# Issue order from a list scheduler, single PSUM banks and matmuls on zeros in a fused attention and MLP kernel

## The chip, the cores and the metric

The kernel runs on one core of one Trainium2 chip. The metric is the device time of one execution in microseconds (us); lower is better. Times are medians of several executions. Ratios are the mean time of one kernel's fast runs over the mean time of the other's in the same rounds, so they are not quite the ratio of the medians quoted beside them. A ratio comes with a 95% interval.

## The reference, cut to what matters

Sliding-window attention with four sink keys (4 batches, 8 heads, 768 positions, head size 64, window 128) is followed by a two-layer MLP (512 to 2048 to 512) with a quick GELU. Inputs and output are float32; the kernel computes in float16 with float32 sums.

```
scores = q @ k.T / 8                       # per head, 768 x 768
keep   = (key < 4) | (0 <= query - key < 128)
attn   = softmax(where(keep, scores, -1e9)) @ v
x      = attn as (4 * 768) x 512
h      = x @ w_in                          # "matmul 1", 512 x 2048
g      = h * sigmoid(1.702 * h)
out    = g @ w_out                         # "matmul 2", 2048 x 512
```

## The kernel before: the parts that matter

The 3072 rows of x are eight slabs of 384. Attention is cut into 32 units: one unit is two heads of one slab, so four units feed a slab and units 0 to 7 feed slabs 0 and 1. A unit has these steps, with the engine of each:

- T: transpose q and k (TensorE), then copy to SBUF. In the first batch T is three 128x384 matmuls against a spreading matrix for each of q and k.
- S: scores A (512 columns per head) and Z (256 or 384 per head) on TensorE, then exp on ScalarE.
- mask: a multiply on VectorE and selects on GpSimd.
- V: probabilities times values (TensorE), then normalise (VectorE).
- X: transpose back (TensorE), copy into xT (VectorE).

Matmul 1 makes h in 16 parts of 128 features per slab; ScalarE's tanh and VectorE's multiply turn each into g. Matmul 2 takes 16 accumulating 128x512 matmuls per 128 rows. Casts from float32 to float16 of q, k, v and of the eight weight blocks w_0 to w_7 run mostly on GpSimd.

The program emits the instructions of each engine in a fixed order, and the traces show the engines keep to it: in the kernel before, GpSimd stands for 8.0 us before unit 4's masks with a cast behind them whose data has landed (below). That order is written by hand: a list for the first batch, then loops.

```python
steps = {
    "T": t_chunk, "S": lambda kk: (s_chunk(kk), mask_chunk(kk)), "V": av_chunk, "X": xt_chunk,
    "c": lambda m: cast_qk(m, (pool, pool)), "v": lambda m: cast_v(m, pool), "w": cast_w,
    "F": lambda f: f_pair(0, f), "G": lambda f: f_pair(1, f),     # matmul 1 of slab 0, slab 1
}
for item in (
    "T0 T1 S0 c1 T2 S1 V0 v1 T3 S2 X0 V1 w0 S3 X1 V2 w1 X2 V3 X3 "
    "F0 F2 c2 v2 F4 T4 S4 T5 F6 S5 c3 V4 v3 T6 X4 V5 S6 T7 X5 w2 S7 V6 w3 "
    "F8 X6 V7 F10 X7 F12 F14 w4 w5 G0 G2 G4 w6 w7 G6 G8 G10 G12 G14"
).split():
    steps[item[0]](int(item[1:]))
```

The eight PSUM banks that the program uses are fixed by purpose: two pairs ("pair", for scores and for two parts of matmul 1), two single banks "misc" and two "out".

```python
def pair(name):
    return psp.tile([P, 2, 512], FP32, tag="pair", name=name)      # two of them

def s_chunk(kk):
    # ... (cut)
    A = pair(f"sA{kk}")
    # ... four score matmuls (cut)
    nc.scalar.activation(out=AT[:, 0:8]..., in_=A, func=AF.Exp, scale=scale)   # both heads at once
    Z = pair(f"sZ{kk}")
    # ... (cut)

def f_pair(n, F):                      # two parts of matmul 1
    if n_f[0] % 3 < 2:
        t = pair(f"hT{n}_{F}")         # one tanh of 128x768 over both
    else:
        hT = [bank("out", f"hT{n}_{F}_{i}", (P, SLAB)) for i in range(2)]
    # ... eight matmuls, tanh, multiply (cut)
```

The softmax here doesn't subtract the row's maximum and nothing guards it: scores larger than these inputs give would overflow.

## Time and profile before

| reading | value | view |
|---|---|---|
| time, median of three runs | 265.0 us | timed runs |
| span of the profiled execution | 261.8 us | page |
| first matmul | 5.8 us | timeline |
| first matmul 1 of slab 0 | 24.6 us | timeline |
| first matmul 1 of slab 1 | 57.8 us | timeline |
| last matmul 2 issued | 257.6 us | timeline |
| ScalarE, VectorE, GpSimd busy | 48%, 50%, 39% | page |

The profile's page is the summary of one profiled execution. PE is TensorE, PEld its weight loads, DVE VectorE, ACT ScalarE, POOL GpSimd, SPq the queue that issues the loads; L and a number is a line of the program, and out<-in names what an instruction writes and reads.

The page of the kernel before, part 1 (busy time by engine) and the lines of part 2 for TensorE and its granted clock. Each digit is one fortieth of the span, 6.5 us, in tenths.

```profile
PE 233.5 (89%) x2048; PEld 132.4 (51%) x2048; DVE 129.8 (50%) x236; ACT 124.7 (48%) x184; POOL 101.6 (39%) x173
...
PE   1585867789989999999799999998999999999994
...
PEclk9987795999999999999999999999999999999999
```

TensorE is near 9 from the ninth slice on and well below in the first eight. The clock line dips in the same place: the clock records behind it stand at 0.5 from 12.0 to 15.4, 22.2 to 29.1 and 39.3 to 46.1 us. The loads move 331 GB/s from 6 to 33 us, with the DMA engines busy all that time (a share of 1.1 in the windows view), and 21 GB/s from 33 to 40 us.

The waits of TensorE in the kernel before. The columns are the waiting tile, the releasing engine and tile, then total us, number of waits and the longest.

```profile
PE tqk_0_163 L177 <- DVE qk_0_153 L147: 5.8, 1, 5.8
PE tqk_0_203 L177 <- POOL qk_1_199 L147: 2.9, 1, 2.9
PE tqk_0_522 L177 <- POOL qk_3_492 L147: 1.9, 1, 1.9
PE sZ_475 L198 <- ACT AT_468 L207: 1.5, 1, 1.5
PE hT_10_0_689 L312 <- DVE xT_79 L296: 1.4, 1, 1.4
```

All the long ones lie before 58 us. The fourth one: a score matmul (sZ) waits for an exp to hand back one of the two PSUM pairs.

The timeline of GpSimd in the kernel before (start, duration, instruction, and in brackets the idle time before it with its releaser).

```profile
26.27 0.83 POOL L154 CAST v_2_392<-v_2_117 128x768 f16<-128x768 f32 x1
35.09 0.77 POOL L252 TENSOR_SCALAR_AFFINE_SELECT AT_421<-AT_421 128x256 f16<-128x256 f16 x2 [7.99 <-ACT AT_421 L225]
39.16 0.77 POOL L252 TENSOR_SCALAR_AFFINE_SELECT AT_468<-AT_468 128x256 f16<-128x256 f16 x2 [3.30 <-ACT AT_468 L225]
39.88 1.60 POOL L147 CAST qk_3_492<-qk_3_123 128x768 f16<-128x768 f32 x2
...
47.44 1.89 POOL L95 CAST w_in_76<-w_2_130 128x2048 f16<-128x2048 f32 x1
```

GpSimd stands for 8 us behind the masks of unit 4 and for 3 us behind those of unit 5. The casts of q/k block 3 (landed about 24 us) and of weight block w_2 (issued at 21.8 us, 8.2 us to landing) wait their turn behind those masks, until 39.9 and 47.4 us.

### The profile page before, as it was taken

The numbers are of one execution on the slowest core, as the hardware profiler recorded it, in microseconds if no ns is written. First come the engines' busy times: TensorE is split into PE (matmuls) and PEld (weight loads), VectorE is DVE, ScalarE is ACT, GpSimd is POOL, SyncE is SP. The second block draws the span as 40 slices with busy tenths as digits, with TensorE's granted clock in tenths as the row PEclk, the third lists the DMA queues.
The fourth block names the chain that finished last, engine by engine and source line by source line (L and its number), as shares of the span: only waits on it lengthen the run. The fifth ranks groups of instructions, "written<-read, shape, count | busy, mean of one in ns | idle before, by whom it ended". The sixth has DMA issues, their size and how long they took to land.

```text
span 261.8 us, 5104 instructions
## 1 busy us (share of the span) xinstructions
PE 233.5 (89%) x2048; PEld 132.4 (51%) x2048; DVE 129.8 (50%) x236; ACT 124.7 (48%) x184; POOL 101.6 (39%) x173
## 2 busy tenths in 40 slices
PE   1585867789989999999799999998999999999994
PEld 0243444446545555666355555655555556654441
DVE  6255443557537543577645434677454434764000
ACT  3371472546455651656456452656555435663111
POOL 6549114875456762166612450375313520000000
PEclk9987795999999999999999999999999999999999
DMA  7999910299997111899711113999311111000222
GB/s 190 306 359 281 385 38 3 81 319 247 226 222 197 44 43 40 204 204 229 127 43 40 43 43 103 228 213 224 62 62 41 42 43 40 3 0 0 83 80 81
DMA packets 75720, 34.12 MB, mean 130 GB/s; under 512 B 64176, under 2 KB 68656, under 8 KB 75696
## 3 DMA queue, kind: packets, MB, share of 16 engines
q1 hardware_dynamic: 75552, 33.76, 50.8%
q8 instruction: 16, 0.26, 0.4%
q14 instruction: 8, 0.07, 0.1%
q10 hardware_dynamic: 144, 0.03, 0.1%
HBM read 27.49 MB, written 6.29 MB: 129 GB/s over the span
## 4 chain that ended last, share of the span: by engine, by line
PE 68%; SPq 6%; POOL 3%; DVE 2%; ACT 2%; DMA 1%; issue 1%; ACTq 0%; POOLq 0%
SPq L126 6%; PE o_2_1031 L332 1%; PE o_0_2607 L332 1%; PE o_2_2743 L332 1%; PE o_2_1907 L332 1%; PE o_4_2945 L332 1%; PE o_4_2109 L332 1%; PE o_0_1771 L332 1%; PE o_3_2846 L332 1%; PE o_1_2660 L332 1%; PE o_3_2010 L332 1%; PE o_1_1824 L332 1%; PE o_5_3444 L332 1%; PE o_2_3384 L332 1%; PE o_5_1420 L332 1%; PE o_4_3424 L332 1%
## 5 line engine op out<-in xcount | busy, mean ns | idle before, releaser
L312 PEld LDWEIGHTS <-w_in_76 128*128 128x128 f16 x512 | 50.5, 99 | 35.9 <-issue 3.9
L332 PEld LDWEIGHTS <-gT_93 128*128 128x128 f16 x48 | 4.7, 98 | 5.7
L332 PEld LDWEIGHTS <-gT_92 128*128 128x128 f16 x48 | 4.7, 98 | 5.5
L177 PE MATMUL tqk_0_163<-spread,qk_0_153 128*128 128x384 f16 x3 | 1.1, 519 | 5.8 <-DVE qk_0_153 L147 5.8
L147 POOL CAST qk_8_1479<-qk_8_1468 128x768 f16<-128x768 f32 x2 | 1.7, 826 | 10.6 <-DMA qk_8_1468<-in_q_dram 9.7
L332 PEld LDWEIGHTS <-gT_86 128*128 128x128 f16 x48 | 4.0, 98 | 3.4
L332 PEld LDWEIGHTS <-gT_90 128*128 128x128 f16 x48 | 3.9, 97 | 3.3
L332 PEld LDWEIGHTS <-gT_88 128*128 128x128 f16 x48 | 3.9, 98 | 3.3
L147 POOL CAST qk_12_2312<-qk_12_2301 128x768 f16<-128x768 f32 x2 | 1.7, 827 | 9.6 <-DMA qk_12_2301<-in_q_dram 8.6
L332 PEld LDWEIGHTS <-gT_89 128*128 128x128 f16 x48 | 3.9, 97 | 2.8
L332 PEld LDWEIGHTS <-gT_91 128*128 128x128 f16 x48 | 3.9, 97 | 2.8
L177 PEld LDWEIGHTS <-qk_0_153 128*128 128x128 f16 x12 | 1.5, 133 | 7.4 <-DVE qk_0_153 L147 5.7
L332 PEld LDWEIGHTS <-gT_87 128*128 128x128 f16 x48 | 3.8, 98 | 2.6
L332 PE MATMUL o_2_1031<-w_out_77,gT_86 128*128 128x512 f16 x16 | 4.5, 380 | 0.0
L332 PE MATMUL o_3_1157<-w_out_77,gT_87 128*128 128x512 f16 x16 | 4.5, 380 | 0.0
L332 PE MATMUL o_4_1301<-w_out_77,gT_87 128*128 128x512 f16 x16 | 4.4, 380 | 0.0
L332 PE MATMUL o_1_937<-w_out_77,gT_86 128*128 128x512 f16 x16 | 4.3, 380 | 0.0
L332 PE MATMUL o_4_2945<-w_out_77,gT_91 128*128 128x512 f16 x16 | 4.3, 380 | 0.0
L332 PE MATMUL o_4_2109<-w_out_77,gT_89 128*128 128x512 f16 x16 | 4.3, 380 | 0.0
L332 PE MATMUL o_2_2743<-w_out_77,gT_90 128*128 128x512 f16 x16 | 4.3, 380 | 0.0
L332 PE MATMUL o_2_1907<-w_out_77,gT_88 128*128 128x512 f16 x16 | 4.3, 380 | 0.0
L332 PE MATMUL o_1_1824<-w_out_77,gT_88 128*128 128x512 f16 x16 | 4.3, 380 | 0.0
(1009 smaller groups left out, 685.3 us busy)
## 6 DMA issues: line engine op xcount, KB each, us to landing
w_0_112<-in_moe_w_in_dram SPq DMA_DIRECT2D x1, 1024.0 KB, 6.7
w_1_114<-in_moe_w_in_dram SPq DMA_DIRECT2D x1, 1024.0 KB, 8.3
w_2_130<-in_moe_w_in_dram SPq DMA_DIRECT2D x1, 1024.0 KB, 8.2
w_3_132<-in_moe_w_in_dram SPq DMA_DIRECT2D x1, 1024.0 KB, 9.6
w_4_134<-in_moe_w_out_dram SPq DMA_DIRECT2D x1, 1024.0 KB, 10.2
w_5_136<-in_moe_w_out_dram SPq DMA_DIRECT2D x1, 1024.0 KB, 5.0
w_6_138<-in_moe_w_out_dram SPq DMA_DIRECT2D x1, 1024.0 KB, 5.6
w_7_140<-in_moe_w_out_dram SPq DMA_DIRECT2D x1, 1024.0 KB, 8.2
```

The costliest lines, as they stand in the source:

```text
L126: nc.sync.dma_start(dst[:, i], s[b, hs, ti : ti + P].rearrange("h s d -> s h d"))
L147: eng(dst, src)
L177: nc.tensor.matmul(tp, qk[:, t, i], spread[:, i], start=(i == 0), stop=(i == NB - 1))
L312: nc.tensor.matmul(hT[i], w_in16[:, c, bass.ts(F + i, P)], xT[n][:, c], start=(c == 0), stop=(c == NHP - 1),)
L332: nc.tensor.matmul(ops, gT[2 * b + j][:, F, bass.ts(i, P)], w_out16[:, F], start=(F == 0), stop=(F == NF - 1))
```

## The change

The intent is to keep TensorE fed in the head. A list scheduler inside the kernel replaces the hand order. Each operation has an engine, a duration, operands and a rank; the scheduler simulates the engines at build time and the kernel emits in the order that results. PSUM becomes eight interchangeable single banks, each unit's A and Z take two each, and matmul 1 runs one part at a time with its own tanh and multiply. Four casts also change engine: k of block 0 goes from ScalarE to GpSimd, q of blocks 1 and 3 from GpSimd to VectorE, k of block 3 from GpSimd to ScalarE. Where the plan shows TensorE idle before 17 us, matmuls on zeros are put in; the intent is to hold the clock up. The diff, cut to its core:

```diff
+class Plan:
+    LAG = {"PE": 0.2, "SP": 1.6}      # time from an operation's end to its result, us
+    def op(self, name, eng, dur, emit, after=(), opens=(), uses=(), rank=0.0, at=0.0, starts=()): ...
+    def order(self, idle):            # always start the operation that can start first,
+        ...                           # ties by rank; slots (banks, buffers) are taken and freed
-    def pair(name):
-        return psp.tile([P, 2, 512], FP32, tag="pair", name=name)
+    slots = dict(ps=8, qk32=4, v32=4, w32=3, qk16=4, v65=6, qkT=8, AT0=2, AT1=2, xnat=2, th=3, ...)
-        A = pair(f"sA{kk}")
-        nc.scalar.activation(out=AT[:, 0:8]..., in_=A, func=AF.Exp, scale=scale)
+        A = [new(f"A{kk}_{h}", (P, 512), FP32) for h in range(2)]
+        for h in range(2):
+            op(f"EA{kk}_{h}", "ACT", 0.5, lambda h=h: e_a(h), ...)
-    def f_pair(n: int, F: int):
+    def add_f(n: int, F: int):        # one part: F (matmuls), H (tanh), G (multiply)
+        op(f"F{nm}", "PE", 0.655, f_mm,
+           after=[f"Xc{4 * n + 3}", f"W{F // 4}"] + ([f"F{n}_{F - 1}"] if F else []), ...)
-    cast_qk(0, (dve, act))
+    add_casts(0, "DVE", "POOL", "POOL")
+    add_casts(1, "DVE", "POOL", "POOL")
+    add_casts(2, "POOL", "POOL", "POOL")
+    add_casts(3, "DVE", "ACT", "POOL")
+    def idle(eng, start, gap):
+        if eng != "PE" or gap < 0.25 or start < 1.3 or start > plan.blank_end:
+            return None
+        return 0.22, lambda: nc.tensor.matmul(
+            T["blank"], idle_in[:, 0:P], idle_in, start=True, stop=True
+        )
+    plan.blank_end = 17.0
+    for _, _, _, emit, _ in plan.order(idle):
+        emit()
... (cut: the same operations as before, wrapped in op(...))
```

The order of instructions, which a build shows without running, has the casts of w_2 and w_3 on GpSimd after the masks of units 4 and 5, unit 4's transposes and scores before and between the first parts of matmul 1, and 17 matmuls on zeros, all after the first real transpose.

## The prediction

> What bounds the kernel now. The windows view shows two regimes. From 57.8 us (first matmul of slab 1) to 257.9 us TensorE is busy almost without a break; its idle slices there sum to about 4.5 us. Before 57.8 us it is starved. Start-to-start times in the timeline price its work: four matmul-1 parts 0.65 us, a 128x512 matmul-2 0.216 us, and per attention unit 0.34 (transposes), 0.17, 0.23, 0.15 to 0.38, 0.39 to 0.55 us. With 0.98 us for the early transposes, the first 57.8 us hold only about 27.5 us of full-speed work: 30 us are lost. The waits view names the pieces: 5.8 us for the first cast, 2.9 and 1.9 us for GpSimd casts of the next q/k, 1.5 us for a PSUM pair behind an exp, 1.4 us for xT. GpSimd itself idles from 27.1 to 35.1 us, while the cast of w_2, landed at 30 us, runs only at 47.4 us; loads w_5 to w_7 stand behind those casts until 49 to 54 us.
>
> Clock: the records show 0.5 around 12.0-15.4, 22.3-29.1 and 39.3-46.2 us; the first sixteen matmul-1s took 4.8 us instead of 2.6. [...] About 5 us are lost so.
>
> What changes. (1) Order: the list scheduler casts weights as they land, starts unit 1 before unit 2's casts, and fills the head with matmul 1 of slab 0, then slab 1 beside unit 8 on. (2) Single PSUM banks: more, smaller ScalarE work. One 128x1024 exp is 1.03 us, a 128x512 one 0.60; tanh 0.81 for a pair, 0.48 single. I estimate +15 us of ScalarE busy (125 to about 140), VectorE about level. Neither is the limit, so this costs nothing on the path. (3) 17 matmuls on zeros, 0.22 to 0.43 us each, all after the first real transpose: none warms the clock before 5.8 us, and the first two may delay unit 0 by up to 1 us. They remove the half-clock dip near 12-15 us.
>
> What stays: the loads keep their order and saturate the DMA to 33 us, so w_2 cannot land much before 30 us. GpSimd's new order puts unit 5's masks behind w_2's cast, about 32.7 us. Following the order with trace durations I expect the first slab-0 matmul 1 near 22.5 us (24.6 before) and all 27.5 us of head work done by about 44 us instead of 57.8: gain 14 us. Unit 8's transposes may stall 1.5 us for w_7 and q/k casts.
>
> After that about 194.5 us of TensorE work remain (155.6 matmul 1 and 2, 24 units at 1.6). I allow 4.5 us of waits, where before took 200. The tail (3.9 us) stays. Span 44+194.5+4.5+3.9 = 247 us; run times lie 2 to 3 us above the span.
>
> Predicted 249 us, range 242 to 256. Chances: faster 0.94, same 0.05, slower 0.01.
>
> Right if: slab 1's matmul 1 starts at 41-47 us; TensorE idle after that under 5 us; clock records have no 0.5 in 12-20 us; ScalarE busy 135-145 us with TensorE no longer waiting on exp; matmul work unchanged. Wrong if: a static order that misjudges DMA or GpSimd times makes TensorE wait behind one late operand (unit 5's masks, matmul 1 on w_2, unit 8), each several us and perhaps at half clock; or ScalarE's smaller pieces hold PSUM banks so that TensorE waits in the steady part.

The sum came to 44 + 194.5 + 4.5 + 3.9 = 247 us of span and, with 2 us added, to 249. The "about 5 us" lost to the clock is no term of it, but an estimate from the half-clock records, in which the trace has TensorE busy for 13.6 of 17.1 us.

## The result and the profile after

The changed kernel takes 249.0 us (four runs, 248.2 to 250.1) against 264.8 us (four runs, with the three of the 265.0 above); the ratio is 0.9395 with an interval of 0.9344 to 0.9446. The prediction was 249.

The page of the changed kernel, the same lines as before:

```profile
PE 231.7 (94%) x2065; PEld 132.8 (54%) x2065; DVE 135.8 (55%) x282; ACT 132.0 (53%) x291; POOL 102.1 (41%) x171
...
PE   0996999989999699999999999999999999999993
...
PEclk9998999999999999999999999999999999999999
```

In the head only the first and the fourth slice, of 6.2 us each, are still low; the zeros count as busy. TensorE's instruction count grew by the 17 zeros. ScalarE's went from 184 to 291 instructions, but its busy time rose only from 124.7 to 132.0 us.

The waits of TensorE in the changed kernel; columns as before.

```profile
PE tp L324 <- DVE qk L265: 6.0, 1, 6.0
PE av L461 <- POOL AT L420: 2.5, 3, 1.9
PE xt L484 <- DVE xn L470: 0.9, 1, 0.9
PE av L461 <- DVE AT L414: 0.8, 1, 0.8
PE tp L346 <- POOL qk L270: 0.8, 1, 0.8
...
PE hT L507 <- ACT AT L388: 0.2, 1, 0.2
```

The first wait, for the first load and cast, is unchanged. The waits for casts of q/k in the head fell from 2.9 and 1.9 us to 0.4 us (not copied), and a wait for an exp is down to 0.2 us.

The timeline of GpSimd in the changed kernel:

```profile
28.03 0.77 POOL L420 TENSOR_SCALAR_AFFINE_SELECT AT<-AT 128x256 f16<-128x256 f16 x2 [3.76 <-ACT AT L394]
28.74 0.15 POOL L279 MEMSET v<- 128x12 f16 x1
28.78 0.83 POOL L280 CAST v<-v 128x768 f16<-128x768 f32 x1
29.55 1.89 POOL L253 CAST w_in<-w 128x2048 f16<-128x2048 f32 x1
32.22 0.77 POOL L420 TENSOR_SCALAR_AFFINE_SELECT AT<-AT 128x256 f16<-128x256 f16 x2 [0.78 <-ACT AT L394]
32.94 1.89 POOL L253 CAST w_in<-w 128x2048 f16<-128x2048 f32 x1
```

The masks of unit 4 come at 28.0 us instead of 35.1, and w_2 is cast at 29.6 us instead of 47.4.

The timeline of TensorE in the changed kernel around the start of slab 1:

```profile
24.10 1.48 PE L507 MATMUL hT<-xT,w_in 128*128 128x384 f16 x4
...
44.07 1.03 PE L542 MATMUL o<-w_out,gT 128*128 128x512 f16 x4
...
45.10 1.89 PE L542 MATMUL o<-w_out,gT 128*128 128x512 f16 x8
46.83 2.76 PE L507 MATMUL hT<-xT,w_in 128*128 128x384 f16 x16
```

Slab 0's first matmul 1 starts at 24.1 us, hardly earlier than before (24.6). But slab 1 starts at 46.8 us instead of 57.8, and twelve matmul 2 are done by then that the kernel before did later. At 0.2157 us each (start to start) they are worth 2.6 us, so the head's work is done at 46.83 - 2.59 = 44.2 us. From there to the last matmul 2 it takes 199.0 us, before it took 199.9. The gain in this trace is therefore 13.5 us in the head and about 1 us after it.

This split is used for every kernel below. "Head" is the start of slab 1's first matmul 1, less 0.2157 us for each matmul 2 already started. "Rest" is from there to the start of the last matmul 2. Both are read from the timeline of one profiled execution, so differences of 1 us in them are not to be trusted.

| kernel | median us | ratio to before | head | rest |
|---|---|---|---|---|
| before | 265 | 1 | 57.8 | 199.9 |
| changed | 249.0 | 0.9395 | 44.2 | 199.0 |
| changed, run again (c0) | 249.1 | 0.941 | 44.4 | 198.2 |
| e1: no zeros | 248.4 | 0.938 | 44.2 | 196.9 |
| e2: before, GpSimd's order only | 260.8 | 0.985 | 54.5 | 199.9 |
| e3: before, ScalarE per bank | 273.5 | 1.033 | 61.0 | 206.6 |
| e5: changed, in the old order | 260.6 | 0.983 | 55.9 | 197.7 |
| e6: before, head order by hand | 260.4 | 0.981 | 54.5 | 200.8 |
| e7: e6's order, single banks | 252.9 | 0.954 | 48.3 | 198.5 |
| f1: longer load allowance | 248.4 | 0.9385 | 44.8 | 198.0 |
| f2: scheduled head, old rest | 249.0 | 0.938 | 45.3 | 197.8 |
| f3a: more zeros | 249.4 | 0.940 | 44.5 | 198.2 |
| f3b: casts on ScalarE | 250.3 | 0.943 | 44.7 | 200.4 |
| f4: f2 and f3b | 248.1 | 0.935 | 44.8 | 197.8 |

### The profile page after: what moved, and what is told of

The parts are those of the page before. It is cut to its first block, busy times and chain, and to the rows that moved or that the text cites. A ratio compares the mean times of both kernels' runs of the same rounds, so it can differ in the third digit from the quotient of the medians.

```text
span 247.7 us, 5387 instructions
## 1 busy us (share of the span) xinstructions
PE 231.7 (94%) x2065; PEld 132.8 (54%) x2065; DVE 135.8 (55%) x282; ACT 132.0 (53%) x291; POOL 102.1 (41%) x171
## 4 chain that ended last, share of the span: by engine, by line
PE 72%; DMA 7%; POOL 7%; SPq 7%; ACT 2%; DVE 2%; issue 2%; ACTq 0%; POOLq 0%
PE o L542 30%; PE hT L507 25%; SPq L220 6%; DMA v<-in_v_dram 6%; PE av L461 4%; PE A L356 3%; PE tp L324 3%; PE tp L346 2%; POOL AT L420 2%; PE Z L356 2%; DMA qk<-in_k_dram 2%; PE xt L484 2%; DVE vs L587 1%; POOL w_in L253 1%; POOL v L280 1%
## 5 line engine op out<-in xcount | busy, mean ns | idle before, releaser
L507 PE MATMUL hT<-xT,w_in 128*128 128x384 f16 x512 | 92.6, 328 | 0.2 <-ACT AT L388 0.2
L542 PE MATMUL o<-w_out,gT 128*128 128x512 f16 x384 | 89.2, 379 | 0.0
L520 DVE SCALAR_TENSOR_TENSOR gT<-th,hT 128x384 f16<-128x384 f16 x128 | 67.1, 548 | 35.0 <-ACT th L513 31.6
L513 ACT ACTIVATE th<-hT 128x384 f16<-128x384 f32 x128 | 60.9, 504 | 30.1 <-PE hT L507 27.8
L507 PEld LDWEIGHTS <-w_in 128*128 128x128 f16 x512 | 47.6, 98 | 29.4 <-issue 1.4
L420 POOL TENSOR_SCALAR_AFFINE_SELECT AT<-AT 128x256 f16<-128x256 f16 (+1 forms) x72 | 35.1, 513 | 56.1 <-ACT AT L394 23.2
L542 PEld LDWEIGHTS <-gT 128*128 128x128 f16 x384 | 35.7, 98 | 38.1 <-issue 0.2
L388 ACT ACTIVATE AT<-A 128x512 f16<-128x512 f32 x64 | 34.7, 595 | 22.1 <-PE A L356 22.1
L394 ACT ACTIVATE AT<-Z 128x256 f16<-128x256 f32 (+1 forms) x64 | 24.8, 452 | 0.0
L270 POOL CAST qk<-qk 128x768 f16<-128x768 f32 x24 | 19.4, 824 | 9.4 <-PE tp L346 3.8
L414 DVE TENSOR_TENSOR AT<-AT,masks 128x1024 f16<-128x1024 f16 x20 | 16.5, 824 | 12.0 <-ACT AT L388 11.9
L356 PEld LDWEIGHTS <-qkT 64*128 64x128 f16 (+1 forms) x384 | 11.5, 93 | 11.9 <-DVE xT L491 3.0
L469 DVE RECIPROCAL rcp<-av 128x6 f32<-128x6 f32 x32 | 6.2, 194 | 17.9 <-PE av L461 17.4
(30 smaller groups left out, 131.4 us busy)
```

The costliest lines, as they stand in the source:

```text
L270: ENG[eng](dst.rearrange("p i h d -> p (i h d)"), src)
L356: nc.tensor.matmul(dst.rearrange("p (t s) -> p t s", s=P), key[hd[h]], qkT(kk)[hd[h], 0, i0 : i0 + ni], start=True, stop=True,)
L388: nc.scalar.activation(out=T[at_][:, 4 * h : 4 * h + 4].rearrange("p a s -> p (a s)"), in_=T[f"A{kk}_{h}"], func=AF.Exp, scale=scale,)
L394: nc.scalar.activation(out=T[at_][:, 8 + SZ[g] * h : 8 + SZ[g] * (h + 1)].rearrange("p a s -> p (a s)"), in_=T[f"Z{kk}_{h}"][:, 0 : SZ[g] ...
L420: nc.gpsimd.affine_select(out=ap, in_=ap, pattern=[[0, ap.shape[1]], [sgn, P]], compare_op=ALU.is_ge if sgn > 0 else ALU.is_gt, fill=0.0, ...
L507: nc.tensor.matmul(hT, w_in16[:, c, bass.ts(F, P)], T[f"xT{n}"][:, c], start=(c == 0), stop=(c == NHP - 1),)
```

## The experiments

Three theories were to be told apart. Theory 1, the prediction's: the order of work in the head makes the gain, and banks and zeros are incidental. Theory 2: the warm clock makes a large part of it. Theory 3: single PSUM banks and one-part matmul 1 make it possible. All kernels gave correct results. The kernels of one batch ran on one chip and shared the runs of the kernel before, whose median lay between 265.0 and 265.4 us in each batch.

### c0: the changed kernel again

> The changed kernel once more, as the yardstick for the runs beside it. Every theory expects 248 to 250.5 us, a ratio to the kernel before near 0.94.

It took 249.07 us, ratio 0.941 (0.938 to 0.944), as expected.

### e1: no matmuls on zeros

```diff
-        return 0.22, lambda: nc.tensor.matmul(
-            T["blank"], idle_in[:, 0:P], idle_in, start=True, stop=True
-        )
+        return 0.22, lambda: None
```

> The changed kernel with the 17 matmuls on zeros left out and the order of everything else kept. Theory 1 (the gain is the order of work in the head): the head is limited by casts, masks and weights landing, so at most 2 us are lost, 249 to 251 us, although the clock records show 0.5 again somewhere between 8 and 20 us. Theory 2 (a large part of the gain is the warm clock): 252 to 255 us.

It took 248.42 us, ratio 0.938 (0.935 to 0.942): no slower than with the zeros, and a little below the range of theory 1. Theory 2 falls as far as it rests on the zeros; a clock that the new order itself keeps up is not tested by this run. The timeline of TensorE without zeros, at the same place as above:

```profile
6.02 2.10 PE L324 MATMUL tp<-spread,qk 128*128 128x384 f16 x6 [6.02 <-DVE qk L265]
...
25.67 0.39 PE L356 MATMUL A<-qkT 64*128 64x256 f16 x4
...
46.80 2.76 PE L507 MATMUL hT<-xT,w_in 128*128 128x384 f16 x16
```

The clock records go to full at 11.9 us here and at 8.8 us with zeros (the four scores of 64x256 took 0.61 us at 8.69 and 0.39 us at 12.12 us here); both have a half-clock window from about 22 to 26 us (three transposes took 1.14 us at 22.1 us here and 1.16 us at 23.1 us with zeros, against 0.65 at full clock). Unit 4's scores start at 25.67 us here and at 25.52 us with zeros, and slab 1 at 46.80 against 46.83. TensorE had slack where the zeros stood. What it has to do there waits for the first units: in this trace 0.57 us for a copy, up to 0.88 us for a normalisation, 0.84 us for a mask, 0.44 us for a cast.

### e2: the kernel before, with only GpSimd's order changed

```diff
-        "T0 T1 S0 c1 T2 S1 V0 v1 T3 S2 X0 V1 w0 S3 X1 V2 w1 X2 V3 X3 "
-        "F0 F2 c2 v2 F4 T4 S4 T5 F6 S5 c3 V4 v3 T6 X4 V5 S6 T7 X5 w2 S7 V6 w3 "
-        "F8 X6 V7 F10 X7 F12 F14 w4 w5 G0 G2 G4 w6 w7 G6 G8 G10 G12 G14"
+        "T0 T1 c1 S0 T2 v1 S1 V0 T3 w0 S2 X0 V1 w1 S3 X1 V2 X2 V3 X3 "
+        "F0 F2 c2 v2 F4 T4 c3 S4 T5 F6 v3 w2 S5 V4 w3 w4 T6 X4 V5 S6 w5 T7 X5 S7 V6 w6 w7 "
+        "F8 X6 V7 F10 X7 F12 F14 G0 G2 G4 G6 G8 G10 G12 G14"
```

Only c, v and w items moved; they are GpSimd's alone, so the other engines keep their order.

> The kernel before, with only GpSimd's order in the head changed: the casts of q/k, v and weights ahead of masks that are not ready yet, as the changed kernel has them. PSUM pairs, matmul-1 pairs and the order of the other engines stay. Theory 1: most of the head gain comes with it, 252 to 257 us, and slab 1's matmul 1 starts near 46 to 50 us. Theory 3 (the gain needs single PSUM banks and matmul-1 parts, which let small pieces fill TensorE): 261 us or more.

It took 260.80 us, ratio 0.985 (0.982 to 0.988), with slab 1 at 54.5 us. Theory 1 expected 252 to 257, theory 3 at least 261: the result lies between and is a miss for the simple form of theory 1. GpSimd's order alone brings 4 us. The timelines of GpSimd and TensorE of e2 say why no more:

```profile
25.95 0.83 POOL L147 CAST qk<-qk 128x768 f16<-128x768 f32 x1 [0.40 <-DMA qk<-in_k_dram]
33.78 0.77 POOL L252 TENSOR_SCALAR_AFFINE_SELECT AT<-AT 128x256 f16<-128x256 f16 x2 [7.00 <-ACT AT L225]
...
35.30 1.90 POOL L95 CAST w_in<-w 128x2048 f16<-128x2048 f32 x1
```

```profile
24.14 5.42 PE L312 MATMUL hT<-xT,w_in 128*128 128x384 f16 x24
29.40 1.14 PE L177 MATMUL tqk<-spread,qk 128*128 128x384 f16 x6
31.55 0.39 PE L198 MATMUL sA<-qkT 64*128 64x256 f16 x4 [1.01 <-DVE qkT L180]
```

Now GpSimd is done with its casts at 26.8 us and stands 7 us for unit 4's masks, because TensorE's own hand order puts 24 matmul 1 before unit 4's transposes. Unit 4's scores come at 31.6 us; in the changed kernel they come at 25.5 us. The orders of the engines hang together.

### e5: the changed kernel's operations and banks, in the old order

The kernel's operations were emitted from an explicit list that repeats the hand order above (each pair of matmul-1 parts as two parts, matmul 2 one matmul at a time), with banks given out in that order and the casts on their old engines. One more buffer for the transposed q and k (eight for seven) stays from the changed kernel. The sequence of matmul shapes on TensorE equals that of the kernel before, all 2048.

```diff
-    for _, _, _, emit, _ in plan.order(idle):
-        emit()
+    # seq: the names of all operations in the order of the kernel before (long list cut)
+    for nm in seq:
+        plan.ops[nm]["emit"]()
```

> The changed kernel's operations, single PSUM banks and one-part matmul 1, emitted in the order of the kernel before, without the scheduler and without matmuls on zeros. Theory 1: nothing of the gain is left, 262 to 267 us; the separate 1.5 us wait of a score matmul for an exp may go. Theory 3: 250 to 257 us.

It took 260.61 us, ratio 0.983 (0.980 to 0.987). Theory 1's range is missed too, and so is theory 3's: the banks and smaller parts bring 4.4 us by themselves, in the traces 1.8 in the head and 2.2 after it. TensorE's waits after the head sum to 4.5 us in the kernel before and to 2.4 us here.

### e6 and e7: the head's order by hand, with pairs and with single banks

e6 is the kernel before with this list; M is the mask, split off from S. e7 is e5 with the same list.

```diff
+        "T0 S0 T1 c1 M0 S1 T2 V0 v1 M1 X0 S2 T3 w0 V1 M2 X1 S3 w1 V2 M3 X2 c2 V3 T4 X3 F0 S4 T5 "
+        "v2 c3 M4 F2 V4 S5 T6 X4 v3 w2 M5 F4 F6 V5 S6 T7 X5 w3 w4 M6 F8 S7 F10 V6 w5 M7 F12 X6 V7 "
+        "F14 w6 w7 X7 G0 G2 G4 G6 G8 G10 G12 G14"
```

> The kernel before (PSUM pairs, matmul-1 pairs, no zeros), with the order of the head on every engine rewritten by hand after the changed kernel's: transposes and scores of unit 4 before matmul 1, masks later, casts as in e2. The steady part is as before. Theory 1, sharpened by e2 (all engines' order together makes the gain, single banks are incidental): slab 1's matmul 1 near 46 to 49 us, 252 to 256 us. Theory 3 (single banks are needed to reach it): 257 us or more, with TensorE waiting for pairs behind exps in the head.

> The same hand order of the head, with the changed kernel's single banks and one-part matmul 1 (as e5, other head). If order and banks add up, 4 us below e6: 248 to 252 us. If the banks only removed waits that the order removes too, the same as e6 within 1.5 us.

e6 took 260.45 us, ratio 0.981 (0.976 to 0.986); e7 took 252.86 us, ratio 0.954 (0.950 to 0.958). The same order is worth 4.6 us with pairs (e6 against the kernel before) and 7.8 us with single banks (e7 against e5); the two changes would add up to 9.0 us and bring 12.2 us together, so 3.2 us come only from the combination. Theory 1's range for e6 is missed, theory 3's is met: single banks are needed to collect all that the order offers. e7 lies 7.6 us below e6, where adding up foretold 4; its range, 248 to 252 us, is missed by 0.9 us. The waits of TensorE in e6:

```profile
PE tqk L177 <- DVE qk L147: 5.7, 1, 5.7
PE xt L294 <- DVE xn L284: 4.2, 7, 0.9
PE sZ L198 <- ACT AT L207: 3.0, 2, 1.5
PE sZ L198 <- DVE gT L319: 2.8, 3, 1.0
```

and in e7:

```profile
PE tp L324 <- DVE qk L265: 5.7, 1, 5.7
PE xt L484 <- DVE xn L470: 4.2, 7, 0.9
PE A L356 <- ACT qkT L329: 1.1, 2, 0.6
```

The first two lines of both are alike. The two sZ lines are gone in e7. Of their 5.8 us, 5.0 us are four waits in the head, where the kernel before has one of 1.5 us; the heads of e6 and e7 differ by 6.2 us. In e6 a Z score needs a PSUM pair, and both are held: one by the A scores that ScalarE is still reading, one by a pair of matmul-1 parts that waits for tanh and multiply. The timeline of e6 shows one such wait:

```profile
29.40 0.39 PE L198 MATMUL sA<-qkT 64*128 64x256 f16 x4
29.50 0.81 ACT L318 ACTIVATE th<-hT 128x768 f16<-128x768 f32 x1 [1.26 <-PE hT L312]
30.21 1.02 ACT L207 ACTIVATE AT<-sA 128x1024 f16<-128x1024 f32 x1
...
31.28 0.23 PE L198 MATMUL sZ<-qkT 64*128 64x128 f16 x2 [1.49 <-ACT AT L207]
```

With matmul 1 threaded more finely between the units this happens four times in the head of e6 and once in that of the kernel before, which fits that the new order gains less with pairs. For this order the two pairs were too few.

Two things blur e6 and e7. The runs of e6 fall into two groups, 257.8 us twice and 260.4 to 261.2 us four times, and the profiled one is the slowest; but even the fast pair is 4.9 us slower than e7. And in the profiled executions the clock stayed at half until 28.1 us in e6 and 20.0 us in e7 (six 128x384 transposes took 2.10 us at 17.4 us in both, and 1.15 us at 31.7 us in e6 and 29.1 us in e7), which blurs them against the changed kernel. It does not explain the difference between the two: unit 4's scores start at 29.40 us in e6 and at 28.52 us in e7, 0.9 us apart, and slab 1 at 54.5 and 48.3 us, 6.2 us apart. From e7 to the changed kernel another 3.9 us go; between the two the order, the engines of four casts and the clock differ, and no run separates these.

### e3: the kernel before, ScalarE one bank at a time, tiles still pairs

```diff
-            groups = [(t[:, :, 0:SLAB], slice(0, 2))]
+            groups = [(t[:, i : i + 1, 0:SLAB], slice(i, i + 1)) for i in range(2)]
-        nc.scalar.activation(out=AT[:, 0:8]..., in_=A, func=AF.Exp, scale=scale)
+        for h in range(2):
+            nc.scalar.activation(out=AT[:, 4 * h : 4 * h + 4]..., in_=A[:, h], func=AF.Exp, scale=scale)
... (cut: the same for Z)
```

> The kernel before, with ScalarE's exps and tanhs one bank at a time (and VectorE's matching multiply), PSUM tiles still pairs. Theory 1: ScalarE busy rises by 7 to 15 us and the time stays at 263 to 267 us. If e5's 4 us came from smaller pieces being handed on earlier, and not from the free assignment of eight banks, it comes here too: 260 to 262 us.

It took 273.53 us, ratio 1.033 (1.029 to 1.037): 8.5 us slower, outside every range. The extra ScalarE work is small, 131.4 us busy instead of 124.7. The loss is a new wait. The waits of ScalarE in e3:

```profile
ACT th L321 <- DVE gT L322: 31.1, 43, 1.2
```

The timelines of ScalarE and VectorE in e3 at one place:

```profile
110.46 0.55 DVE L322 SCALAR_TENSOR_TENSOR gT<-th,hT 128x384 f16<-128x384 f16 x1 [1.47 <-ACT th L321]
...
111.05 1.26 ACT L321 ACTIVATE th<-hT 128x384 f16<-128x384 f32 x3 [0.62 <-DVE gT L322]
```

The second bank's tanh starts only when VectorE's multiply on the first bank ends, at 111.01 us, though it reads another bank. In this program a tile is what engines hand to each other, and the two banks are one tile. In the kernel before, where the two parts lie in two tiles, the second tanh starts at 106.89 us and the multiply of the first at 107.31 us, without such a wait. So smaller instructions alone are not what helped in e5 and e7; without tiles of one bank each they cost more than they give. Whether the free choice among eight banks or the separate tiles weigh more there was not separated.

### f1: a longer allowance for loads

```diff
-    LAG = {"PE": 0.2, "SP": 1.6}
+    LAG = {"PE": 0.2, "SP": 3.2}
```

(and no zeros)

> An attempt at a better version: the changed kernel without zeros, and with the scheduler's allowance from a load's issue to its landing raised from 1.6 to 3.2 us, nearer to the 3.6 us that the profile shows. It should remove the 1.9 us wait for a mask behind a v cast at 84 us: 246 to 249 us. If TensorE's remaining waits cost nothing, 248 to 250 us.

It took 248.39 us, ratio 0.9385 (0.935 to 0.942), the same as e1. The 1.9 us wait went, and the mask waits that remain still sum to 2.3 us over three places. Nothing gained.

### f2: the scheduler for the head only

```diff
+    # seq = order of a Plan that holds only units 0 to 7, slab 0's matmul 1 and the weight casts,
+    # followed by the list of e5 from matmul 1 of slab 1 on (cut)
```

> Single banks throughout; the scheduler orders only the head (units 0 to 7, matmul 1 of slab 0, weight casts); from matmul 1 of slab 1 on, the order is that of the kernel before, as in e5 and e7. No zeros. If the scheduler gains only in the head: TensorE's head work done at 44 us as in the changed kernel, the rest in 197 to 198 us as in e5 and e7, so 246.5 to 249 us. If the scheduler's interleaving in the steady part is worth something by itself: 250 us or more.

It took 248.98 us, ratio 0.938 (0.936 to 0.941), head 45.3 us, rest 197.8 us. Its casts are on the changed kernel's engines. It is as fast as the changed kernel whole: the scheduler's interleaving after the head is worth nothing that these runs can show.

### f3a: zeros for longer

```diff
-    plan.users["blank"].add("Xc3")
+    plan.users["blank"].add("SA4")
-    plan.blank_end = 17.0
+    plan.blank_end = 23.0
```

> The changed kernel with zeros allowed until 23 us of the plan instead of 17 (10 more), to take away the half clock that the records show from 22.5 to 25.9 us. If that half clock costs what the timeline suggests (transposes of unit 4 at 0.96 us instead of 0.48, the first matmul-1 part at 1.2 instead of 0.65): 247 to 248 us. If what follows waits for casts and loads anyway, as e1 showed for the earlier zeros: 248.5 to 249.5 us, with slab 1's matmul 1 at 46.8 us again.

It took 249.44 us, ratio 0.940 (0.938 to 0.942). The clock records go to full at 11.7 us, 2.9 us later than in the changed kernel, and show no half-clock window after that (the mean granted clock of the profiled execution is 1.00; three transposes take 0.66 us at 23.5 us, where the changed kernel's took 1.16 at 23.1 us); slab 1 starts at 47.07 us. This run is not a clean proof that the half clock near 22 us is free. In its trace the scores of unit 2 start at 16.2 us, 1.3 us later than in the changed kernel, and unit 4's scores start at 25.70 us all the same. What it does show is that a head at full clock from 11.7 us on is no faster in the end.

### f3b and f4: unit 4's casts on ScalarE

```diff
-    add_casts(2, "POOL", "POOL", "POOL")
+    add_casts(2, "ACT", "ACT", "POOL")
```

f3b is this in the changed kernel without zeros; f4 is this in f2.

> The changed kernel without zeros, with the casts of unit 4's q and k on ScalarE, idle then, instead of GpSimd, which gets to them 1.2 us after k lands. If unit 4 is what TensorE waits for near 22 us, its transposes start about 1 us earlier and the time falls to 247 to 248 us; otherwise 248 to 249 us as e1.

> f2 and f3b together, an attempt at the best version: 245.5 to 248 us if both gains hold; no better than f2 if unit 4 is not the limit.

f3b took 250.32 us, ratio 0.943 (0.941 to 0.946): a miss, about 0.5% slower than e1. Its first matmul 1 starts at 27.0 us instead of 24.4; in its order unit 4's scores and unit 5's transposes come before it. Its head still ends at 44.7 us, and its rest takes 200.4 us, the longest of the scheduled kernels; why was not followed up. It is no matter of the clock, whose records show no half after 18.2 us (the mean granted clock of the profiled execution is 1.00). f4 took 248.10 us, ratio 0.935 (0.933 to 0.938). That is the lowest median of all, 0.4% below the changed kernel and beside f2 (0.936 to 0.941) not clearly apart. All variants with single banks and a scheduled head lie between 248.1 and 250.3 us.

## Why the prediction was right, point by point

- **The head.** Predicted: all head work done at about 44 us, slab 1 at 41 to 47 us. Measured: 44.2 us, slab 1 at 46.8. Expected for GpSimd: unit 5's masks behind w_2's cast at about 32.7 us. Measured: cast at 29.55, masks at 32.22 us.
- **The rest.** Predicted 199 us (194.5 of work and 4.5 of waits). Measured 199.0 in this trace; 196.9 to 198.2 in c0, e1 and f3a, which have the same order but for zeros. Idle after slab 1's start, without the tail, is about 3.5 us (201.17 us of window less 193.23 busy and 4.4 of tail).
- **The sum of the gain came out for a reason that the prediction told only in half.** That it fell on 249 is in part luck: the first matmul 1 came 1.6 us later than predicted and the head still ended on time, the tail took 4.5 us and not 3.9, and the profiled run lay 1.7 us above its span and not 2 to 3. The prediction gave all of the 14 us to the order, and said of the single banks that they cost "nothing on the path", only as added ScalarE work. The runs: GpSimd's order alone 4.2 us (e2), the head's order on all engines with pairs 4.6 us (e6), single banks alone 4.4 us (e5), order and banks together 12.2 us (e7), with the scheduler's order and cast engines 16 us. By costing only what the banks add, I missed that they take away the wait for a pair. It was even in the list of waits (1.5 us for "a PSUM pair behind an exp"), and I did not ask how often it would come with matmul 1 threaded more finely.
- **ScalarE's busy time.** Predicted 140 us (135 to 145), measured 132.0. The step that failed is "one 128x1024 exp is 1.03 us, a 128x512 one 0.60", summed as if durations add up. They overlap: two 128x512 exps back to back span 1.08 us in the changed kernel's timeline, only 0.05 more than one of 128x1024. The order has a part in it: in e5, in the old order, the same number of ScalarE instructions kept it busy for 137.4 us.
- **The clock.** Predicted: about 5 us lost to it before, and zeros that remove the dip near 12 to 15 us. The dip is gone (full from 8.8 to 22.5 us), and of the one from 22.2 to 29.1 us a stretch from 22.5 to 25.9 us is left. The zeros are worth nothing: e1 without them is no slower (248.4 us against 249.1 in c0), so in the changed kernel slow early matmuls were not lost time. For the kernel before this stays open, because no run changed its clock alone. Its trace has matmul 1 in half clock from 24.6 us (eight in 2.56 us from start to start, against 1.30 us at 55.2 us), unit 4's transposes following without a wait at 30.7 us, and GpSimd idle until unit 4's masks; so part of what the order gains may be the clock, whose records at half sum to 17.1 us in the head before and to 3.4 us in that of the changed kernel. The runs do not separate this.
- **The start.** Predicted: first matmul 1 of slab 0 near 22.5 us. Measured 24.1, in the half-clock window from 22.5 to 25.9 us. The gain lies between 24 and 47 us, where TensorE is now busy 22.66 of 22.73 us.
- **Unit 8** waits 0.8 us for its cast; predicted 1.5.

## What to carry to other kernels

When several in-order engines feed each other, an operation that stands too early in one engine's queue holds back everything behind it (here GpSimd for 8 us); read each engine's idle time together with what stood ready behind the wait, and move the orders of all engines together, since one engine's alone brought a quarter here. A finer interleaving needs buffers that can be taken and returned one at a time: before judging an order, count which buffers each step holds, because the same order was worth 4.6 us with two PSUM pairs and 7.8 us with eight single banks. Splitting instructions without splitting the tile they work on can cost more than it gives (8.5 us in e3), and matmuls on zeros, meant to hold the clock up, bought nothing here (249.1 us with them, 248.4 without), where TensorE had other things to wait for.

## What the traces show of the clock, and of VectorE beside GpSimd

- In the two main traces each record of the granted clock, but for the last, lasts a multiple of 3.41 us: 3.41, 6.83, 10.24 and 215.0 us in the kernel before, 3.41, 13.65 and 221.9 us in the changed kernel.
- Rises. In the 3.41 us before a record of full clock began, TensorE was busy for 83, 84, 100 and 100% in the kernel before (at 8.6, 15.4, 29.1 and 46.1 us) and for 82 and 100% in the changed kernel (at 8.8 and 25.9 us). In e6 TensorE counted as busy for 8.54 of the 10 us from 10 to 20 us (at half clock) and stayed at half until 28.1 us: counted back from there in steps of 3.41 us, five stretches were 71 to 83% busy, and the one before the rise 94%. In e7, with the same head, the stretch before the rise at 20.0 us was busy throughout. These traces show no single share of busy time at which the clock rises.
- Falls. The clock fell to half after 3.41 us in which TensorE was busy for 33, 42 and 44% in the kernel before (at 12.0, 22.2 and 39.3 us), for 45% in e7 (at 23.4 us) and for 37% in the changed kernel: at 22.48 us, after 1.25 us busy of 3.41, with no gap above 0.9 us. Filling gaps bought nothing: 248.4 us without and 249.1 us with the 17 matmuls on zeros, and 249.4 us in f3a, which had no such fall.
- The granted clock of a profile reads 1.00 before the first record. In the kernel before it does so from 5.2 to 8.6 us, while three 128x384 transposes took 1.14 us at 5.75 us, as they did at 12.56 us in a record of 0.5, and 0.65 us at 15.75 us. In e6 it reads 1.00 in every window up to 200 us, while six of these transposes took 2.10 us at 17.4 us and 1.15 us at 31.7 us.
- In the changed kernel VectorE's mask multiply took 0.68 us alone (at 27.5 us) and 1.26 us at 17.2 and 19.8 us, where it met a weight cast on GpSimd; the GpSimd select beside it took 0.85 us instead of 0.41. What the two engines wait for there the traces do not show.
